# Fused attention and mixer: x and u turned by DMA transposes instead of TensorE matmuls, one DMA transpose for q and k of a pair, other quotas

## The chip, the cores and the metric

The kernel runs on one core of a Trainium2 chip. The metric is the device time of one execution in microseconds (us). The engines have short names in the profile: PE is TensorE (matmuls), PEld its weight loads, DVE is VectorE, ACT is ScalarE, POOL is GpSimd and SP is SyncE, which issues DMAs. POOL issues DMAs too. Sixteen DMA engines serve all queues.

## What is computed

Eight batches (b = 0 to 7), eight heads, 576 tokens, head width 64. Causal attention over 16 beacon keys and 576 keys gives x of shape 8 x 576 x 512; x then goes through a mixer over tokens and a two-layer MLP:

```
scores = q @ k_all.T / 8, masked;  a = softmax(scores);  x = a @ v_all
h = x.T @ U @ V                      # U: 576 x 32, V: 32 x 576, over tokens
u = x + h.T
out = u + relu(u @ w_ch1) @ w_ch2    # 512 -> 2048 -> 512
```

Inputs and output are float32; the kernel works in float16 with float32 sums in PSUM.

## The kernel before

**Attention.** A *pair* is two heads of one batch: p = 4b + c, with c = 0 to 3, so 32 pairs. For a pair, `regroup` (L216) copies q and k on DVE into a tile `pr`, tokens on the partitions. From batch 3 on (`HB = 3`), `turn_pair` (L248) has SP turn these with two DMA transposes, one for k and one for q, into `raw`, and `order_units` (L256) copies each on DVE into its place in `qT` and `kT`. For the batches before, `qkT_units` turns them on PE (L229, L231). `score_units` makes the scores in two visits of PE (L286), each followed by exps on ACT (L292), and then the masks on DVE (L273, L275). `av_unit` multiplies with v (L310) and writes x, scaled, into `xb` on DVE (L318, L319): tokens on the partitions, 5 groups of 112, 128, 128, 128 and 80 tokens by 512 channels.

**Mixer.** The MLP needs u with channels on the partitions, the tile `uT` (4 chunks `cc` of 128 channels by all 4608 tokens). `mix_units` (L323) gives a `head` (x times U, L339) and two `part`s, of 240 and 336 tokens. A part fills four PSUM tiles `ups`, one for each cc. When `turned` is false, 20 matmuls a batch with the identity put x itself, turned, into `ups` (L354), four matmuls with V add h (L364), and the sum is copied into `uT`, two copies on ACT (L374) and two on DVE (L372). When `turned` is true, DMA transposes (L324) have written x into `uT` before, the 20 matmuls fall away, and all four results are added to `uT` on DVE (L370).

`mix(b)` sets `turned` to `b >= NF and len(queue) >= LAG + 5`, with `NF = 2` and `LAG = 12`. At the calls the queue holds 12, 8, 7, 6, 5, 4 and 3 units for b = 1 to 7, so it is false each time: all eight batches go through the identity.

**MLP.** `uT` is cut into nine blocks of 512 tokens. `mlp_units` (L378) gives 32 units of four matmuls for a block: 16 `g_unit`s (first layer, L397, with a relu on ACT or DVE) and 4 x 4 `c_unit`s (second layer, L413). The residual u needs tokens on the partitions again: four DMA transposes of `uT` into `ut` (L387), issued at the first g unit, and an add on DVE (L426). For block 0, `turned` is false: u is added by 16 identity matmuls (L421), and the result is copied by DVE (L430) and ACT (L428).

**Order of the work.** It is written out by hand (`tc.manual_schedule`): each engine works through its instructions in the order in which the Python code emits them. Attention is emitted pair by pair; between its seven steps `fill` pops units from a queue of MLP and mixer units, evenly, `quota` of them in a pair (9; 4 in batch 2, by `QUOTA`). `feed(b)` appends the blocks that batch b completes. `mix(b)` puts the mixer units ahead of them: the first `LAG` units of the queue when `turned` (2 or none otherwise), the head, up to three units, the first part, up to three units, the second part, up to three units. For b = 0 and 1 `mix(b)` is called behind the last pair of the batch, for b = 2 to 6 at the first pair of the next batch, for b = 7 at the end; behind pair 7 (the end of batch 1) come 16 units with no attention between them (`AHEAD`). What is still in the queue after pair 31 runs as a tail of MLP alone.

So a batch's last pair, its mixer and the first MLP block that needs it follow each other in one stream on PE, and a late `uT` holds up the first `gps` matmul of that block.

**Queues.** SP issues in order: the outputs (L431, each waits for the DVE's or ACT's `ob`), the transposes of q and k (L244 once a batch, L253 twice a pair) and those of u (L387). POOL issues the loads of q, k and v, which convert float32 to float16 and are cut into small packets: v of the next batch as soon as the last pair of a batch has released its buffer, and q and k of two batches ahead right behind.

Of the kernel before, what the change touches and what calls it, by code (L numbers as in the profile page):

```python
# [17 lines left out]
P = 128  # L18
# [9 lines left out]
def kernel(  # L28
# [187 lines left out]

    def regroup(L, c, i, copy):

        t = pairs.tile([P, 4, 2, D], F16, name=f"pr{i}", tag=f"pr{i}")
        copy(out=t, in_=by_token(L[1][i][:, 2 * c : 2 * c + 2, :]))  # L220
        return t

    def qkT_units(L, pr, qT, kT, c):
# [3 lines left out]
        def one(i, dst, w):  # L227
            ps = pst([P, SK], F16, name="tps")
            nc.tensor.transpose(ps[:, 0:NL], L[0][i][:NL, hs, :], ident[:NL, :NL])  # L229
            for j in range(4):  # L230
                nc.tensor.transpose(ps[:, ds(NL + P * j, P)], pr[i][:, j, :, :], ident)  # L231
# [16 lines left out]
    def turn_pair(pr):  # L248

        out = []  # L250
        for i in range(2):
            t = raws.tile([P, 4, P], F16, name=f"raw{i}", tag=f"raw{i}")
            nc.sync.dma_start_transpose(out=t, in_=pr[i].rearrange("p j h d -> p (j h d)"))  # L253
            out.append(t)
        return out

    def order_units(raw, qT, kT, c):

        def one(i, dst, w):
            nc.vector.tensor_copy(  # L260
                out=dst[:, c, w - 4 * P : w].rearrange("x (p j) -> x p j", j=4),
                in_=raw[i].rearrange("x j p -> x p j"),
            )
# [42 lines left out]
    def av_unit(b, h, ex, vs, xb):  # L306
# [14 lines left out]
        )  # L321

    def mix_units(xb, u0, turned=True):  # L323


        cell = {}

        def turn():
            for j in range(NT):
                nc.sync.dma_start_transpose(  # L330
                    out=uT[:, :, ds(u0 + q0[j], nq[j])], in_=xb[: nq[j], j, :]
                )

# [41 lines left out]

        return turn, head, [lambda: part([0, 1]), lambda: part([2, 3, 4])]

# [126 lines left out]
    def group_first(c, i, copy):  # L504

        prs.setdefault(c, []).append(regroup(Ls[0], c, i, copy))
        hs = SETS[c]
        copy(out=Ls[0][0][i][:NL, hs, :], in_=raw["head"][:NL, i, hs, :])

    def regroup_of(p):  # L510
        b, c = divmod(p, NH2)
        prs[p] = [regroup(Ls[b], c, i, nc.vector.tensor_copy) for i in range(2)]

# [45 lines left out]
    AHEAD = 16  # L559
    LAG = 12  # L560
    HINT = 5

    FIRST = [0, 0, 0, 0, 10, 5, 4, 4]

    QUOTA = {2: 4}

# [35 lines left out]
    with tc.manual_schedule(engines={ENG.PE, ENG.Activation, ENG.DVE, ENG.SP, ENG.Pool}):  # L602
# [41 lines left out]
        for p in range(NP1):  # L644
# [37 lines left out]
        for p in range(NP1, NP):  # L682
# [84 lines left out]
    with tc.If(n_bad != 0, label="general"):  # L767
        with tc.For_i(0, B, 1) as bi:
# [4 lines left out]
            for c in range(NH2):  # L773
                pr = [regroup(L, c, i, nc.vector.tensor_copy) for i in range(2)]
# [4 lines left out]
            _, head, parts = mix_units(xb, 0, False)  # L779
            head()  # L780
# [36 lines left out]
```

## Time and profile before

| | us |
|---|---|
| median of 3 runs (lowest to highest) | 368.31 (367.41 to 369.45) |
| the profiled execution | 367.15 |
| its span in the profile | 365.5 |
| outside the span | 1.65 |
| PE busy | 349.8 |
| MLP matmuls, L397 and L413, busy | 135.7 + 134.4 |
| x through the identity on PE, L354, busy | 11.6 (160 matmuls) |
| copies of `ups` to `uT`: DVE L372, ACT L374 | 13.1, 11.5 |

The page's busy times are unions: a matmul's own duration (379 ns for 512 columns) overlaps the next one's, so the time that matmuls take in the stream is read from the start of one group to the start of the next in the timeline. In the timeline each row is a run of like instructions: start, length, engine, line, operation, out<-in, count, and in brackets the idle time ahead of it with what ended it. The table of stretches gives for each stretch the busy time of each engine and the granted share of the TensorE clock (PEclk).

### The profile page before, as it was taken

Reading aid. Unit: us, or ns where it says so; the run is one execution under the profiler, and the core shown is the slowest. Engines: PE = TensorE matmul, PEld = TensorE weight load, DVE = VectorE, ACT = ScalarE, POOL = GpSimd, SP = SyncE. Lnnn points to the kernel's source line nnn. Section 1 sums busy time; section 2 is a strip of 40 time slices with the busy share of each in tenths; the row PEclk is TensorE's granted clock in tenths of the full one; section 3 lists DMA queues with packets and bytes.
Section 4 is the critical chain, followed back from the end, with each engine's and each line's share of the span. In section 5 each row is a group of like instructions: output and inputs, shape, how many; then the busy total and the mean of one; then the engine's idle time right before and its main releaser. Section 6 shows DMA issues by size and latency. Waiting matters only on the chain.

```text
span 365.5 us, 7721 instructions
## 1 busy us (share of the span) xinstructions
PE 349.8 (96%) x3040; PEld 173.5 (47%) x3040; DVE 204.7 (56%) x565; ACT 173.7 (48%) x382; POOL 83.9 (23%) x123
## 2 busy tenths in 40 slices
PE   7777999999999999999999999999999999999995
PEld 3544545545545444544445444544454555444442
DVE  4887664357776675565666666756566446223311
ACT  3976660177654553466436643674356503401300
POOL 8976436400336001800081005000000000000000
PEclk9989999999999999999999999999999999999999
DMA  9999999990999952999299917942141013013112
GB/s 178 212 151 184 194 201 156 176 170 10 145 136 163 178 80 59 121 190 137 60 111 206 131 35 101 150 74 41 63 120 26 2 57 103 14 59 87 31 44 79
DMA packets 117916, 40.52 MB, mean 111 GB/s; under 512 B 93680, under 2 KB 112112, under 8 KB 117872
## 3 DMA queue, kind: packets, MB, share of 16 engines
q0 software_dynamic: 65904, 17.54, 54.4%
q1 hardware_dynamic: 51520, 22.12, 31.0%
q8 instruction: 25, 0.41, 0.5%
q10 hardware_dynamic: 448, 0.30, 0.3%
q14 instruction: 19, 0.16, 0.1%
HBM read 37.86 MB, written 9.44 MB: 129 GB/s over the span
## 4 chain that ended last, share of the span: by engine, by line
PE 85%; DMA 6%; DVE 3%; ACT 2%; POOL 2%; issue 0%; DVEq 0%; POOLq 0%
PE cps L413 34%; PE gps L397 33%; PE po L310 6%; PE sps L286 6%; DMA w<-in_moe_w_ch_dram 2%; DMA raw<-pr 2%; PE ups L354 2%; DMA st<-in_q_dram 2%; ACT expt L292 2%; PE idle L211 1%; POOL vs L173 1%; DVE gT L403 1%; PE ups L364 1%; PE qtp L339 1%; PE tps L231 1%; DVE expt L273 1%
## 5 line engine op out<-in xcount | busy, mean ns | idle before, releaser
L292 ACT ACTIVATE expt<-sps 128x496 f16<-128x496 f32 (+2 forms) x256 | 111.1, 531 | 61.9 <-PE sps L286 61.7
L397 PE MATMUL gps<-uT,w 128*128 128x512 f16 x576 | 135.7, 379 | 1.8 <-ACT uT L374 1.2
L413 PE MATMUL cps<-w,gT 128*128 128x512 f16 x576 | 134.4, 379 | 0.0
L401 ACT ACTIVATE gT<-gps 128x512 f16<-128x512 f32 x86 | 51.8, 608 | 64.3 <-PE gps L397 62.0
L413 PEld LDWEIGHTS <-gT 128*128 128x128 f16 x576 | 52.3, 98 | 61.1 <-issue 3.7
L397 PEld LDWEIGHTS <-w 128*128 128x128 f16 x576 | 51.8, 98 | 60.8 <-issue 6.1
L403 DVE TENSOR_SCALAR gT<-gps 128x512 f16<-128x512 f32 x58 | 40.1, 691 | 45.7 <-PE gps L397 44.0
L426 DVE TENSOR_TENSOR ob<-cps,ut 128x512 f32<-128x512 f32 x32 | 22.1, 691 | 49.6 <-PE cps L413 49.1
L173 POOL DMA_DIRECT2D vs<-in_v_dram x50 | 40.8, 831 | 14.3 <-DMA st<-in_q_dram 4.9
L310 PEld LDWEIGHTS <-expt 128*128 128x128 f16 (+1 forms) x960 | 36.9, 98 | 15.0 <-DVE expt L273 2.2
L310 PE MATMUL po<-vs,expt 128*128 128x65 f16 (+1 forms) x960 | 40.3, 195 | 1.0 <-DVE expt L273 0.5
L286 PE MATMUL sps<-qT,kT 64*128 64x80 f16 (+4 forms) x384 | 33.4, 286 | 4.0 <-DVE kT L233 3.4
L319 DVE TENSOR_TENSOR xb<-po,rec 128x320 f16<-128x320 f32 x64 | 31.4, 491 | 2.2
L374 ACT ACTIVATE uT<-ups 128x240 f16<-128x240 f32 (+1 forms) x32 | 11.5, 416 | 39.3 <-PE ups L364 39.2
L273 DVE TENSOR_TENSOR expt<-expt,bigmask 128x512 f16<-128x512 f16 x64 | 26.7, 418 | 6.0 <-ACT expt L292 5.9
L163 POOL DMA_DIRECT2D vs<-in_beacon_v_dram x10 | 5.4, 538 | 100.6 <-PE po L310 100.3
L318 DVE RECIPROCAL rec<-po 128x5 f32<-128x5 f32 x64 | 12.0, 187 | 27.0 <-PE po L310 26.2
L286 PEld LDWEIGHTS <-kT 64*128 64x128 f16 x384 | 12.3, 95 | 30.1 <-issue 10.8
L372 DVE CAST uT<-ups 128x240 f16<-128x240 f32 (+1 forms) x32 | 13.1, 450 | 8.5 <-PE ups L364 8.5
L220 DVE COPY pr<-st 128x512 f16<-128x512 f16 x56 | 14.2, 296 | 1.0 <-DMA st<-in_q_dram 0.6
L260 DVE COPY qT<-raw 128x512 f16<-128x512 f16 x20 | 12.4, 619 | 2.7 <-DMA raw<-pr 2.7
L275 DVE TENSOR_TENSOR expt<-expt,mask 80x80 f16<-80x80 f16 x64 | 12.5, 196 | 0.0
(65 smaller groups left out, 157.2 us busy)
## 6 DMA issues: line engine op xcount, KB each, us to landing
out_dram<-ob SPq DMA_DIRECT2D x36, 256.0 KB, 2.3
w<-in_moe_w_ch_dram POOLq DMA_DIRECT2D x4, 1024.0 KB, 11.5
st<-in_k_dram POOLq DMA_DIRECT2D x6, 512.0 KB, 10.0
st<-in_q_dram POOLq DMA_DIRECT2D x6, 512.0 KB, 13.4
vs<-in_v_dram POOLq DMA_DIRECT2D x18, 128.0 KB, 7.5
stm<-in_k_dram SPq DMA_DIRECT2D x4, 256.0 KB, 4.6
vs<-in_v_dram POOLq DMA_DIRECT2D x12, 64.0 KB, 6.2
stm<-in_q_dram SPq DMA_DIRECT2D x3, 256.0 KB, 5.7
```

What stands on the lines that cost most here:

```text
L173: nc.gpsimd.dma_start(out=dst[a : a + nq[j], j, :, :], in_=src[hs, ds(q0[j], nq[j]), :].rearrange("h p d -> p h d"))
L220: copy(out=t, in_=by_token(L[1][i][:, 2 * c : 2 * c + 2, :]))
L273: nc.vector.tensor_tensor(out=e4, in0=e4, in1=bigmask, op=ALU.min)
L286: nc.tensor.matmul(ps[g, i][:, ds(o, w)], kT[hp, c, ds(P * ch, P)], qT[hp, c, ds(qa, w)], start=True, stop=True,)
L292: nc.scalar.activation(out=ex[i][:, ds(SLOT * g, gw[g])], in_=ps[g, i][:, 0 : gw[g]], func=AF.Exp, scale=scale)
L310: nc.tensor.matmul(po[:, j, :], ex[0 : nk[c], ds(blk[(c, j)], P)], vs[0 : nk[c], ds(c * H * E + h * E, E)], start=(c == 0), stop=(c == j),)
L319: nc.vector.tensor_tensor(out=xb[:, :, ds(h * D, D)], in0=po[:, :, 0:D], in1=r.broadcast_to([P, NT, D]), op=ALU.mult)
L397: nc.tensor.matmul(g[:, 0:n], w1[:, cc, ts(dc, P)], uT[:, cc, ds(t0, n)], start=(cc == 0), stop=(cc == NCC - 1))
L401: nc.scalar.activation(out=gT["t"][:, dc, 0:n], in_=g[:, 0:n], func=AF.Relu)
L403: nc.vector.tensor_scalar_max(out=gT["t"][:, dc, 0:n], in0=g[:, 0:n], scalar1=0.0)
L413: nc.tensor.matmul(ps[:m, :], gT["t"][:, dc, ds(P * i, m)], w2[:, dc, :], start=(dc == 0), stop=turned and dc == NDC - 1, skip_group_check ...
L426: nc.vector.tensor_tensor(out=ob[:m, :], in0=ps[:m, :], in1=gT["u"][:m, i, :], op=ALU.add)
```

## The change

Four things, told with the lines of the kernel before where there are such:

- `mix(b)` sets `turned = b > 0`. For b = 1 to 7 x is turned by ten DMA transposes from SP: five (one for each token group) of channels 0 to 383, issued behind the third pair of the batch, and five of channels 384 to 511, issued in `mix(b)`. `LAG` is 8. The two parts' results are added to `uT` on DVE.
- Block 0 takes u from DMA transposes as the others do.
- q and k of a pair share one tile `pr` and one DMA transpose of 128 x 1024, in place of two of 128 x 512.
- The quota is 6 in batch 3 and 8 in batch 7 (4 in batch 2 as before, else 9).

```diff
-    def regroup(L, c, i, copy):
-        t = pairs.tile([P, 4, 2, D], F16, name=f"pr{i}", tag=f"pr{i}")
-        copy(out=t, in_=by_token(L[1][i][:, 2 * c : 2 * c + 2, :]))
-        return t
+    def pair_tile():
+        return pairs.tile([P, 2, 4, 2, D], F16, name="pr", tag="pr")
+    def regroup(L, c, i, copy, pr):
+        copy(out=pr[:, i, :, :, :], in_=by_token(L[1][i][:, 2 * c : 2 * c + 2, :]))
...
     def turn_pair(pr):
-        out = []
-        for i in range(2):
-            t = raws.tile([P, 4, P], F16, name=f"raw{i}", tag=f"raw{i}")
-            nc.sync.dma_start_transpose(out=t, in_=pr[i].rearrange("p j h d -> p (j h d)"))
-            out.append(t)
-        return out
+        t = raws.tile([P, 2, 4, P], F16, name="raw", tag="raw")
+        nc.sync.dma_start_transpose(
+            out=t.rearrange("x i j p -> x (i j) p"), in_=pr.rearrange("p i j h d -> p (i j h d)")
+        )
+        return t
...
+    def turn_x(xb, u0, c0, c1):
+        for j in range(NT):
+            nc.sync.dma_start_transpose(
+                out=uT[:, c0:c1, ds(u0 + q0[j], nq[j])], in_=xb[: nq[j], j, P * c0 : P * c1]
+            )
...
-    LAG = 12
+    LAG = 8
-    QUOTA = {2: 4}
+    QUOTA = {2: 4, 3: 6, 7: 8}
...
-                mlp_units(512 * t, 512, lambda i, m, t=t: rows[ds(512 * t + P * i, m), :], t % 2, t > 0)
+                mlp_units(512 * t, 512, lambda i, m, t=t: rows[ds(512 * t + P * i, m), :], t % 2)
...
-        turned = b >= NF and len(queue) >= LAG + 5
-        turn, head, parts = mix_units(xbs[b], S * b, turned)
+        turned = b > 0
+        head, parts = mix_units(xbs[b], S * b, turned)
         if turned:
-            turn()
-        n = LAG if turned else 2 if b >= NF else 0
+            turn_x(xbs[b], S * b, NH2 - 1, NH2)
+        n = LAG if turned else 0
...
+            if c == NH2 - 2 and b > 0:
+                turn_x(xbs[b], S * b, 0, NH2 - 1)
...
+            if c == NH2 - 2:
+                turn_x(xbs[b], S * b, 0, NH2 - 1)
```

The first of the last two places is in the loop over the pairs of batches 0 and 1, the second in the loop over the others.

More of the change, by code (lines that the diff above doesn't have):

```diff
@@ L261, in one @@
                 out=dst[:, c, w - 4 * P : w].rearrange("x (p j) -> x p j", j=4),
-                in_=raw[i].rearrange("x j p -> x p j"),
+                in_=raw[:, i, :, :].rearrange("x j p -> x p j"),
             )
@@ L374, in part @@
                     nc.scalar.activation(out=dst, in_=ups[cc], func=AF.Copy)
-        return turn, head, [lambda: part([0, 1]), lambda: part([2, 3, 4])]
+        return head, [lambda: part([0, 1]), lambda: part([2, 3, 4])]
     def mlp_units(t0, n, dst, flip, turned=True):
@@ L504, in group_first @@
     def group_first(c, i, copy):
-        prs.setdefault(c, []).append(regroup(Ls[0], c, i, copy))
+        if c not in prs:
+            prs[c] = pair_tile()
+        regroup(Ls[0], c, i, copy, prs[c])
         hs = SETS[c]
@@ L511, in regroup_of @@
         b, c = divmod(p, NH2)
-        prs[p] = [regroup(Ls[b], c, i, nc.vector.tensor_copy) for i in range(2)]
+        prs[p] = pair_tile()
+        for i in range(2):
+            regroup(Ls[b], c, i, nc.vector.tensor_copy, prs[p])
     for i in range(2):
@@ L773 @@
             for c in range(NH2):
-                pr = [regroup(L, c, i, nc.vector.tensor_copy) for i in range(2)]
+                pr = pair_tile()
+                for i in range(2):
+                    regroup(L, c, i, nc.vector.tensor_copy, pr)
                 for u in qkT_units(L, pr, qT, kTs[0], c):
@@ L778 @@
                 safe_head(h, qT, kTs[0], vss[0], xb)
-            _, head, parts = mix_units(xb, 0, False)
+            head, parts = mix_units(xb, 0, False)
             head()
```

7 lines of the change are left out of this document (1 added, 6 removed).

## The prediction

> **What bounds the kernel.** I read the page's head first, then its 40 slices, then who waited for whom, then the timelines of PE, DVE and SP around the mixer of a batch.
>
> ```profile
> span 365.5 us, 7721 instructions
> PE 349.8 (96%) x3040; PEld 173.5 (47%) x3040; DVE 204.7 (56%) x565; ACT 173.7 (48%) x382; POOL 83.9 (23%) x123
> PE   7777999999999999999999999999999999999995
> DMA  9999999990999952999299917942141013013112
> ```
>
> PE is busy 96% of the span. The table of stretches says where the rest lies: 8.8 us before 34.9 us, 4.1 us behind the last attention pair (297 us on, nearly all of it the end), 2.7 us in the 262 us between. So from 35 to 297 us a matmul taken off PE's stream is worth its full place in the stream, and any wait put into it costs in full. DVE and ACT have room on the mean. The DMA engines do not: up to about 210 us they are busy most of the time (9 is 90% or more).
>
> What x costs on PE is read from the timeline of PE, batch 4's mixer:
>
> ```profile
> 191.94 0.60 PE L354 MATMUL ups<-ident,xb 112*128 112x112 f16 x8
> 192.47 0.28 PE L364 MATMUL ups<-Vsb,qts 32*128 32x240 f16 x4
> ...
> 194.03 0.77 PE L354 MATMUL ups<-ident,xb 128*128 128x128 f16 x12
> 194.73 0.32 PE L364 MATMUL ups<-Vsb,qts 32*128 32x336 f16 x4
> ```
>
> From start to start the eight take 0.53 us and the twelve 0.70: 1.23 us a batch.
>
> **What goes.** The built order of the changed kernel has 312 fewer rows on PE: 140 matmuls of L354 and 16 of L421, each with its weight load.
> - L354 for b = 1 to 7: 7 x 1.23 = 8.6 us.
> - L421: in the same timeline four of them stand at 59.60 and what follows at 59.92 or, at the other three places, 0.22 us later (69.18 to 69.40). 4 x 0.22 = 0.9 us.
> - Two waits of `gps` for `uT`, at 119.33 (0.53 us) and 158.11 us (0.67), 1.2 us in all by PE's waits. Both belong to the form in which a part stands right ahead of the block that needs it; I count them off here and set the new waits in full below.
>
> All of it lies on PE's full stretch: -10.7 us. The ACT copies that go (L374, 7 x 4) and the halved count of `raw` transposes free engines that do not bound: nothing. The identity transposes of q and k for batches 0 to 2 stay. The quotas move units between batches and the tail (70 units in the queue at the end before, 86 after); PE is full in both, so nothing, as long as a pair with six units still covers ACT (four exps of 1.96 us and four of 1.53 us, about 3.5 us) and DVE. With PE at 6 x 0.87 + 2.3 us = 7.5 us a pair it does; batch 2 already runs with four.
>
> **What is added on DVE.** All eight adds of a batch are now DVE's. Two copies of 240 take 0.71 us together there, two of 336 take 0.92, so one more costs 0.32 and 0.42 us: four adds take 1.3, then 1.7 us. (An add that reads PSUM and SBUF takes what a copy does: L426 691 ns for 512, L430 the same.) On the mean DVE stays under 65%. But two batches have no units left between the parts and the next block's first g unit, and there the chain of adds lies on the path:
> - b = 1 (no attention beside it). The queue gives: part 0, c unit, part 1, g1.0. From the end of part 0 on PE: DVE adds 1.3, the `ob` add 0.6, the adds of part 1 1.7, so the last is done at 3.7 and g1.0 ends at 4.0; undisturbed it ends at 0.87 + 0.25 + 0.94 = 2.1. Cost 2 us.
> - b = 2, pair 13, quota 6: second score visit, head, masks, part 0, k's order copy, part 1, av, g2.0. DVE has the masks ahead of the adds, and the masks wait for four exps (1.6 us behind the visit). Then 0.9 masks, 1.3, 0.5, 1.7: the last add at 6.0, g2.0 ends at 6.2. Undisturbed: 0.4 + 0.22 + 0.25 + 0.46 + 0.94 = 2.3. Cost 4 us.
> - b = 3 to 6: nine and more units between part 1 and the g unit, b = 7 five. The adds are covered: nothing.
>
> The rows in which DVE shows this order today, ahead of the wait at 119.33 (DVE's timeline):
>
> ```profile
> 112.84 0.41 DVE L273 TENSOR_TENSOR expt<-expt,bigmask 128x512 f16<-128x512 f16 x1
> ...
> 114.24 0.71 DVE L372 CAST uT<-ups 128x240 f16<-128x240 f32 x2
> ...
> 118.86 0.92 DVE L372 CAST uT<-ups 128x336 f16<-128x336 f32 x2
> ```
>
> **What is added on SP and the DMA engines.** Ten transposes a batch, 35 KB to 98 KB each. No row shows an issue of 128 or 384 channels, or of 1024. Every issue of 512 columns takes 1.2 us on SP, with 64 rows (L244) as with 128, and lands 2.4 us after its start where the DMA engines are idle. Either the columns set it (0.3, 0.9, 2.4 us) or each takes 1.2; I take half way for the last five (0.65, 3.3 us for five), 1 us for the first. Landing beside POOL's loads is much later, and POOL loads v exactly when a batch's last pair has ended, which is when SP issues the last five:
>
> ```profile
> L253 SPq DMA_TRANSPOSE raw<-pr x2: 1276/1276/1277, 146.5 to 147.9; - x2
> DMA to landing us min/median/max: 7.6/8.5/9.5
> ```
>
> This is the tile `raw` asked for alone at 146 to 150 us; at 107 to 111 us it is 6.4 to 7.0, at 185 to 188 us 5.3 to 6.6, from 264 us on 2.4.
> - When are they due? b = 3: part 0's adds come eight units, the head, three units and most of two pairs' attention behind, 13.7 us after pair 16 starts; part 1's 18.5. The issue of the first two ends at about 1 (regroup) + 2 (raw) + 1.3 = 4.3, plus 8.5 to 9.5 landing: 13 to 14. Just in time; b = 4 to 6 have shorter landings, b = 7 no loads.
> - b = 1: last x at 58.5 us, issue done by 62.2, landing 4 to 6.7 (what `ut` and `ob` take at 60 to 80 us): 66 to 69; part 0 is due at 68. b = 2: the adds are held to about 119 and 121 us by the masks anyway, x lands 118 to 122. I set 0.5 us for all of them together; the bounds are 0 and the 3 us by which a landing of 12 us would be late at each of b = 1 to 5.
> - Pair 14's `raw` stands on SP behind the first five of b = 2 (issued at about 102.7 us, when xb is ready): 102.8 now, 107.7 then, landed 111 to 113, while DVE's order copy comes at 109.4 and has masks and k's copy behind it, which pair 13's scores need. Pair 13 begins at 113.4 and needs them at 2.5 us behind the landing, 113.5 to 115.5: 1 us (bounds 0 and 3). Later batches have a pair of 10 us to cover this.
> - Single transposes for q and k save SP nothing or 1.2 us a pair, and DVE's q copy waited for the second one before as well: nothing.
>
> **A cold clock.** The longest idle time of PE behind its start-up is 1.56 us (before 22.65 us), and the clock falls behind it:
>
> ```profile
> 18.00:22.00 4.00, 2.53 (x44) 1.59 (x43) 3.33 (x11) 3.51 (x9) 2.55 (x5) 1.00 1.60 183
> 22.00:26.00 4.00, 3.35 (x39) 1.89 (x39) 3.58 (x13) 1.84 (x6) 3.52 (x6) 0.69 1.50 140
> 26.00:30.00 4.00, 3.21 (x60) 2.24 (x56) 3.25 (x12) 2.97 (x8) 4.00 (x10) 0.89 1.14 106
> ```
>
> (start and end, length, busy time of PE, PEld, DVE, ACT, POOL, then PEclk.) 4 x 0.31 + 4 x 0.11 = 1.7 us of clock lost. The new wait at b = 2 is longer than that one, but PE is full ahead of it: I set half, 0.8 us; bounds 0 and 2 x 1.7.
>
> The Trainium skill, "TensorE: Matmul & The Clock Gate", Part 1 (What's actually happening), gives a rule for it: the array falls to half its clock after one idle window of about 3.4 us. By it only b = 2's wait would be long enough, and only if av does not break it; the row above, with 1.56 us idle, speaks for an earlier fall than the rule. By the rule the sum would be 0.8 us lower, by the row 0.9 us or more higher.
>
> **The sum.** -10.7 + 2 + 4 + 0.5 + 1 + 0.8 = -2.4 us. The profiled execution's own 367.15 (span 365.5 and 1.65 around it) would become 364.75, the median of 368.31 becomes **365.9 us**, 0.65% less. The start, the end and what lies around the span stay.
>
> **The rivals.**
> - *The new waits are smaller than worked out.* If g2.0 does not wait the whole chain out, or the clock holds and nothing is late, -10.7 + 2 + 2 to 4 leaves 361.5 to 363.7; I set 362.5. For it: DVE has idle time beside every part; against it: the built order has masks ahead of the adds.
> - *x lands late in the loaded windows, and DVE, which works in order, stands still with masks, `ob` and relus behind the add.* This is the case that ends slower. Its place is b = 2 to 5, the pairs beside POOL's loads; it decides from a landing of 9.5 us for the second of the last five, which is what `raw` shows today at 147.9 us, without 2304 more packets a batch behind and beside it. Another 512 or so in the same window, at the pace of the two above (1.9 us more landing for the second), put x at about 12 us: 3 us late, at four batches, 12 us: 365.9 + 12 = 378 us; with only two batches late 372. For it: the DMA row at 9; against it: the loads end about 20 us into a batch, and 8 to 11 units lie between.
> - The Trainium skill, "DMA: Bandwidth & Descriptors", Queues, rings and completion order, says that each DMA engine takes turns between queues by packets, so transposes go on beside a full load queue at a share of the pace. The landings of 5 to 10 us against 2.4 agree; a share, not a full wait, speaks against the 378.
> - *That the change does not do it* (`turned` false, as before) is excluded by the 312 rows.
>
> **How the numbers follow.** Forecast 0.50 (364 to 368.5: six tenths of it over 0.5% faster, the rest within); smaller waits 0.25 (faster); late landings 0.25 (slower in all but a tenth). 0.5%, 1.8 us, is about what a measurement of this kernel can tell from no change. So faster 0.54, same 0.23, slower 0.23. The range is 361.5 to 374: it leaves out the late landings at three and more batches, and the case with no wait at all (357.6).
>
> **What would show it.** L354 at 20 matmuls and L421 gone. PE waits at g1.0 (about 2 us) and g2.0 (about 4 us) for the DVE add into `uT`, near 69 and 119 us; PEclk below 1 behind the latter. `uT<-xb` landings of 6 to 10 us at the start of batches 3 to 6, and adds that wait for them by less than 1 us. PE full from 130 us on, 1.2 us a batch shorter. It is wrong if DVE waits for `uT<-xb` by microseconds in several batches, or if g2.0 does not wait.

## The result, and the profile after

The changed kernel takes 380.82 us (379.23 to 381.68, 4 runs), the kernel before 367.90 on the same chip: a ratio of 1.034, with an interval of 1.029 to 1.039. It is slower by 12.9 us; the forecast was 365.9, the range 361.5 to 374.0. The times of this document are medians over all executions, while the ratios leave out executions over 1.5% slower than the fastest of their kernel. The profiled execution took 380.61 us with a span of 378.9.

Line numbers of the changed kernel differ a little: L326 issues the transposes of x, L252 those of `raw`, L388 those of `ut`; L371 adds into `uT`, L260 copies `raw` into order, L340 and L346 make `qts`, L365 adds h; L398 and L414 are the two MLP layers, L286 the scores, L310 a @ v, L427 the `ob` add.

The head of the page and three rows of its 40 slices (PE, the clock, the DMA engines), to be laid beside those of before:

```profile
span 378.9 us, 7523 instructions
...
PE 349.6 (92%) x2884; PEld 167.0 (44%) x2884; DVE 216.3 (57%) x596; ACT 162.3 (43%) x351; POOL 83.6 (22%) x123
...
PE   7677998689996789999999999999999999999995
...
PEclk9999999969999669999999999999999999999999
...
DMA  9999999999999963999599939553422312203202
```

PE does 156 matmuls less and is as long busy as before (349.6 against 349.8 us). A busy time that stays while work goes means a slower clock, and the row PEclk shows it: a 6 in slice 9, two in slices 14 and 15, each behind a slice (8 and 13) in which PE has a 6. The balance of the span closes: the matmuls removed are worth 8.6 + 0.9 = 9.5 us by the prediction's rows; PE's busy time fell by 0.2, so the clock cost 9.3; PE's idle time rose from 15.7 to 29.3 us, 13.6 more. -9.5 + 9.3 + 13.6 = +13.4 us, from 365.5 to 378.9. From slice 16 on both rows are clean. (The 9.5 are of the prediction's rows, so the 9.3 is an estimate, and the highest of three; the other two, 6.6 and 7.8, are worked out below.)

The table of stretches of the changed kernel says the same in four rows (columns as before: start and end, length, PE, PEld, DVE, ACT, POOL with counts, PEclk, DMA share, GB/s):

```profile
34.90:73.10 38.20, 35.75 (x305) 17.49 (x306) 19.04 (x51) 11.61 (x25) 10.12 (x13) 1.00 1.75 162
73.10:106.70 33.60, 29.59 (x258) 14.27 (x257) 23.34 (x70) 19.04 (x42) 12.15 (x17) 0.90 2.15 152
106.70:145.50 38.80, 31.01 (x273) 14.03 (x272) 22.93 (x65) 15.64 (x35) 8.89 (x11) 0.82 1.18 143
145.50:310.00 164.50, 163.27 (x1409) 77.30 (x1408) 106.14 (x284) 79.86 (x172) 22.04 (x28) 1.00 0.81 109
```

The same stretches of the kernel before:

```profile
34.90:73.10 38.20, 37.66 (x342) 19.49 (x343) 19.42 (x54) 14.12 (x31) 18.17 (x24) 1.00 1.73 183
73.10:106.70 33.60, 32.62 (x321) 16.19 (x320) 23.87 (x73) 23.23 (x51) 4.83 (x8) 1.00 1.07 117
106.70:145.50 38.80, 38.27 (x347) 18.87 (x347) 24.07 (x66) 20.22 (x45) 9.38 (x12) 1.00 1.05 120
```

So nearly everything is lost in two places, at the mixers of b = 1 and b = 2; the mixers of b = 3 to 6 lie in the last row of the changed kernel, at full clock and 99% busy (that of b = 7 begins at 308.58). PE's timeline at the first place, the end of batch 1 (last column: idle time ahead and what ended it):

```profile
72.52 0.32 PE L365 MATMUL ups<-Vsb,qts 32*128 32x336 f16 x4
75.78 1.44 PE L398 MATMUL gps<-uT,w 128*128 128x512 f16 x3 [2.94 <-DMA uT<-xb]
78.52 0.58 PE L398 MATMUL gps<-uT,w 128*128 128x512 f16 x1 [1.30 <-DVE uT L371]
```

and at the second, pairs 12 and 13:

```profile
125.21 0.98 PE L286 MATMUL sps<-qT,kT 64*128 64x496 f16 x4 [5.41 <-DVE kT L260]
...
131.61 1.09 PE L365 MATMUL ups<-Vsb,qts 32*128 32x240 f16 x8 [0.40 <-DVE qts L346]
133.28 0.80 PE L310 MATMUL po<-vs,expt 128*128 128x65 f16 x15 [0.59 <-DVE uT L371]
135.14 1.87 PE L398 MATMUL gps<-uT,w 128*128 128x512 f16 x4 [1.06 <-DVE uT L371]
```

The waits of these six rows make 11.7 us, of 13.6 us of new idle time. The waits for the loads of the MLP weights grew by 2.1: 1.32 us for `w1` at 35 us and 1.33 for `w2` at 59, where the kernel before waits 0.58 for `w1`.

The longest wait, 5.41 us, is not for x at all: it is pair 13's scores waiting for the ordering copies of `raw`. (The code makes scores one pair ahead, `scores_of(p + 1)`: "pair 13's scores" are those made in pair 13's turn, and they belong to pair 14. That is why they need pair 14's `raw`.) DVE's timeline and SP's show why:

```profile
122.57 0.59 DVE L260 COPY qT<-raw 128x512 f16<-128x512 f16 x1 [7.52 <-DMA raw<-pr]
```

```profile
107.93 6.39 SPq L326 DMA_TRANSPOSE uT<-xb  x5
114.43 2.26 SPq L252 DMA_TRANSPOSE raw<-pr  x1
```

Pair 14's `pr` was ready at 107.9 us (its regroup: 107.43, 0.48 us for both copies), but SP was issuing five transposes of x until 114.3; `raw` went out at 114.43 (102.8 in the kernel before; 5.2 us of the difference are the lateness of the whole stream from batch 1 on) and needed 8.1 us to land, at 122.6. DVE stood for 7.52 us with the masks and k's copy behind that instruction, and PE for 5.41. The transposes themselves (the line's rows by operation):

```profile
L326 SPq DMA_TRANSPOSE uT<-xb x70: 1172/1246/2255, 55.6 to 307.2; - x70
```

Smallest, median and largest issue in ns: 128 and 384 channels cost the same 1.25 us (five of 384 take 6.39 us from 107.93 on, five of 128 take 6.46 from 120.13 on). `raw`, now 1024 columns, has a median of 1260 ns, where 512 columns had 1216. So the price of an issue on SP does not go with its size; single issues took up to 2.4 us (`raw`) and 3.4 (`ut`), pair 14's own 2.26.

The gain itself is read from a steady batch, from the first matmul of one head to that of the next. Before it is 38.79 us (188.53 to 227.32), in the changed kernel 38.36 (200.11 to 238.47): 0.43 us less, and not 1.23. The first row is the kernel before, the second the changed one:

```profile
188.53:227.32 38.79, 38.77 (x349) 19.06 (x349) 25.05 (x65) 20.33 (x45) 8.62 (x12) 1.00 1.00 120
200.11:238.47 38.36, 37.93 (x330) 17.91 (x329) 25.38 (x68) 18.80 (x41) 5.08 (x6) 1.00 1.10 138
```

PE's busy time falls by 0.84 us there. At this rate the change takes 7 x 0.84 + 0.9 = 6.8 us of work off PE, and the clock costs 6.6 us. PE's timeline at batch 4's first part:

```profile
204.17 0.48 PE L286 MATMUL sps<-qT,kT 64*128 64x336 f16 x8
204.58 0.28 PE L365 MATMUL ups<-Vsb,qts 32*128 32x240 f16 x3
205.29 0.26 PE L365 MATMUL ups<-Vsb,qts 32*128 32x240 f16 x1 [0.43 <-ACT expt L292]
205.48 2.77 PE L414 MATMUL cps<-w,gT 128*128 128x512 f16 x12
```

The four matmuls that stay take 0.90 us here, where four of L364 took 0.22 in the prediction's timeline: 0.43 us of it is a wait for an exp on ACT, which has to release a PSUM tile; the rest is no wait that the trace names. In the kernel before, the part stands elsewhere: twelve MLP matmuls lie between the score visit and the part's matmuls at 191.94.

```profile
188.93 0.48 PE L286 MATMUL sps<-qT,kT 64*128 64x336 f16 x8
189.34 2.76 PE L413 MATMUL cps<-w,gT 128*128 128x512 f16 x12
```

With `LAG` at 8 the part of batches 4 and 5 falls right behind a score visit, whose exps still run, and no identity matmuls fill the time. In batch 6, where four MLP matmuls lie between (281.41), the four L365 do not wait. No run has one of the two without the other, so what share each has is not shown.

What the waits do to the clock is read from stretches of 4 us:

```profile
120.00:124.00 4.00, 0.00 (x0) 0.00 (x0) 1.43 (x6) 0.00 (x0) 0.49 (x1) 0.91 1.52 210
124.00:128.00 4.00, 2.79 (x22) 1.38 (x23) 2.83 (x9) 1.96 (x4) 0.00 (x0) 0.50 1.46 173
...
136.00:140.00 4.00, 4.00 (x26) 1.55 (x25) 3.08 (x9) 1.96 (x4) 0.00 (x0) 0.50 0.64 98
```

The second 0.50 comes behind the three short waits at g2.0, the first g unit of block 2 (0.40, 0.59, 1.06 us; g1.0 is that of block 1), and PE is full at half clock for 4 us. With the stretches between (0.73 and 0.69), the next one (0.95) and those at the first place (0.50 and 0.71 from 76 to 84 us) the shares missing add up to 2.42 stretches, 9.7 us at the most, as PE was idle in part of them. With each missing share weighted by PE's busy time in its stretch it is 7.8 us. The three estimates put the clock's cost at 6.6 to 9.3 us.

### The profile page after: what moved, and what is told of

It is laid out like the page before. It is cut to its first block, busy times and chain, and to the rows that moved or that the text cites. A ratio compares the mean times of both kernels' runs of the same rounds, so it can differ in the third digit from the quotient of the medians.

```text
span 378.9 us, 7523 instructions
## 1 busy us (share of the span) xinstructions
PE 349.6 (92%) x2884; PEld 167.0 (44%) x2884; DVE 216.3 (57%) x596; ACT 162.3 (43%) x351; POOL 83.6 (22%) x123
## 4 chain that ended last, share of the span: by engine, by line
PE 74%; DMA 14%; DVE 4%; SPq 4%; ACT 2%; POOL 2%; issue 1%; DVEq 0%; ACTq 0%; POOLq 0%
PE gps L398 33%; PE cps L414 27%; PE po L310 6%; PE sps L286 6%; DMA raw<-pr 4%; SPq L326 3%; DMA uT<-xb 3%; DMA w<-in_moe_w_ch_dram 2%; DMA stm<-in_k_dram 2%; DMA st<-in_q_dram 2%; ACT expt L292 1%; DMA stm<-in_q_dram 1%; POOL vs L173 1%; PE tps L232 1%; DVE expt L273 1%
## 5 line engine op out<-in xcount | busy, mean ns | idle before, releaser
L398 PE MATMUL gps<-uT,w 128*128 128x512 f16 x576 | 139.3, 387 | 6.6 <-DMA uT<-xb 2.9
L414 PE MATMUL cps<-w,gT 128*128 128x512 f16 x576 | 135.5, 383 | 1.3 <-DMA w<-in_moe_w_ch_dram 1.3
L402 ACT ACTIVATE gT<-gps 128x512 f16<-128x512 f32 x85 | 51.0, 609 | 110.9 <-PE gps L398 106.8
L398 PEld LDWEIGHTS <-w 128*128 128x128 f16 x576 | 52.8, 99 | 67.1 <-issue 11.8
L414 PEld LDWEIGHTS <-gT 128*128 128x128 f16 x576 | 52.9, 98 | 65.3 <-issue 8.6
L427 DVE TENSOR_TENSOR ob<-cps,ut 128x512 f32<-128x512 f32 x36 | 24.8, 690 | 50.4 <-PE cps L414 50.1
L310 PEld LDWEIGHTS <-expt 128*128 128x128 f16 (+1 forms) x960 | 37.6, 99 | 17.5 <-issue 4.0
L310 PE MATMUL po<-vs,expt 128*128 128x65 f16 (+1 forms) x960 | 40.9, 196 | 2.0 <-ACT expt L292 0.7
L286 PE MATMUL sps<-qT,kT 64*128 64x80 f16 (+4 forms) x384 | 33.6, 287 | 8.8 <-DVE kT L260 5.6
L286 PEld LDWEIGHTS <-kT 64*128 64x128 f16 x384 | 12.2, 94 | 35.6 <-issue 9.8
L371 DVE TENSOR_TENSOR uT<-ups,uT 128x240 f16<-128x240 f32 (+1 forms) x56 | 21.8, 449 | 7.9 <-PE ups L365 4.9
L260 DVE COPY qT<-raw 128x512 f16<-128x512 f16 x20 | 11.9, 595 | 12.5 <-DMA raw<-pr 12.5
L260 DVE COPY kT<-raw 128x512 f16<-128x512 f16 x20 | 12.0, 600 | 0.0
## 6 DMA issues: line engine op xcount, KB each, us to landing
st<-in_k_dram POOLq DMA_DIRECT2D x6, 512.0 KB, 10.3
```

What stands on the lines that cost most here:

```text
L260: nc.vector.tensor_copy(out=dst[:, c, w - 4 * P : w].rearrange("x (p j) -> x p j", j=4), in_=raw[:, i, :, :].rearrange("x j p -> x p j"),)
L286: nc.tensor.matmul(ps[g, i][:, ds(o, w)], kT[hp, c, ds(P * ch, P)], qT[hp, c, ds(qa, w)], start=True, stop=True,)
L310: nc.tensor.matmul(po[:, j, :], ex[0 : nk[c], ds(blk[(c, j)], P)], vs[0 : nk[c], ds(c * H * E + h * E, E)], start=(c == 0), stop=(c == j),)
L398: nc.tensor.matmul(g[:, 0:n], w1[:, cc, ts(dc, P)], uT[:, cc, ds(t0, n)], start=(cc == 0), stop=(cc == NCC - 1))
L402: nc.scalar.activation(out=gT["t"][:, dc, 0:n], in_=g[:, 0:n], func=AF.Relu)
L414: nc.tensor.matmul(ps[:m, :], gT["t"][:, dc, ds(P * i, m)], w2[:, dc, :], start=(dc == 0), stop=turned and dc == NDC - 1, skip_group_check ...
```

## The experiments

Two theories. **Queue:** SP issues in order, x takes ten issues of 1.25 us a batch, and five of them stand ahead of `raw`; the remedy is another order or fewer issues. **Contention:** what is late is the landing, 8 to 11 us beside POOL's loads where 2.4 us is the idle figure; the order matters little, and the remedy is to have no transposes there. The kernel before was timed beside each of the four groups of runs: 367.32, 367.37, 368.59 and 368.47 us. These differ by 1.3 us, so a gain of about a microsecond between runs of different groups is not told from none.

### Which batches: x by DMA from batch 3 on

```diff
-        turned = b > 0
+        turned = b > 2
-        n = LAG if turned else 0
+        n = LAG if turned else 2 if b >= NF else 0
...
-            if c == NH2 - 2:
+            if c == NH2 - 2 and b > 2:
                 turn_x(xbs[b], S * b, 0, NH2 - 1)
```

The first five of b = 1 go too; the rest of the change stays. The edit also puts the mixers of b = 1 and 2 back to their old place, behind 0 and 2 units of the queue in place of 8.

> x of b = 1 and 2 through the identity again, DMA transposes for b = 3 to 7 alone; the other three parts of the change stay. Queue theory (SP issues in order at 1.25 us per transpose whatever its size; the x of b = 1 and 2 comes late itself and holds up raw of pair 14; PE idles 13.6 us more than before and its clock falls for another 9.3): the loss was in b = 1 and 2 alone, so 367.9 - 5 x 1.23 (L354) - 0.9 (L421) - 0.7 (the wait at b = 3) + about 1.9 (w2 later behind u's transposes) = 362 us, mean clock back at 0.99. Contention theory (every added DMA slows all landings in the loaded windows, in batches 3 to 6 as well): 366 us or more.

366.57 us (363.83 to 369.96, 10 runs), ratio 0.995 (0.990 to 0.999). All of the loss is gone, with 2.5 us of matmuls put back; the clock is 1.00 throughout. Some waits remain: for `w1` (1.08 us) and `w2` (1.78 us; the expectations of later runs call both waits those for w2), and, beside 0.51 us for `kT`, this one ahead of pair 16's scores:

```profile
129.77 0.62 PE L310 MATMUL po<-vs,expt 128*128 128x65 f16 x15 [1.37 <-DVE gT L404]
```

So the transposes of the two early batches, with the place of their mixers, are the cause of the loss. The time is the one set for the contention theory, but not for its reason: no instruction of this run waits for x. The 362 us are not reached: the gain of a steady batch is smaller than 1.23 us, as its rows above showed, and these waits stand against it.

### One of the two batches through the identity

The same edit with `turned = b > 1` (b = 1 through the identity), and with `b > 0 and b != 2` (b = 2).

> Only b = 1 goes back to the identity; b = 2 to 7 by DMA transposes. Queue theory: the wait at g1.0 (72.8 to 79.1 us, 5.2 us) and the slow clock behind it (about 3.4 us) go, 1.2 us of identity matmuls come back: 380.8 - 7.4 = 373.4 us; pair 13's wait of 5.4 us stays. Contention theory: the loads of batch 2 and 3 come earlier too and pair 13's wait shrinks as well, 370 us or less.

375.22 us, ratio 1.021 (1.013 to 1.030): 5.6 us come back. The waits at g1.0 are gone, the one ahead of pair 13's scores is still 4.43 us. Here the stream is not late: the five transposes of x go out at 103.26 us, `raw` of pair 14 at 109.90, POOL's loads from 106.94 on, and `raw` lands in 7.8 us.

> Only b = 2 goes back to the identity. Queue theory: raw of pair 14 is issued some 6 us earlier on SP, pair 13's wait (5.4 us), the waits around g2.0 (about 2 us) and the slow clock behind them (6.5 us) go, 1.2 us of identity matmuls come back: 380.8 - 12.7 = 368 us; the wait at g1.0 stays. Contention theory: v of batch 4 loads at that time anyway, raw lands 6 us or more after its issue, half of the wait stays: 374 us.

371.48 us, ratio 1.010 (1.005 to 1.014): 9.3 us come back by the medians (8.9 by the ratios), between the two expectations. The two places add up: 5.6 + 9.3 = 14.9 us, against the 14.3 us of both together (380.82 - 366.57). With 1.23 us of identity matmuls put back at each, the price of b = 1 is about 6.8 us and that of b = 2 about 10.5.

### How much of it is the clock

Matmuls with the identity into an unused PSUM tile keep PE at work where it would wait: 13 ahead of g1.0, 24 ahead of pair 13's scores. What PE waits for stays as it is.

```diff
+        if b == 1:
+            p1 = parts[1]
+            parts[1] = lambda: (p1(), keep_warm(pst([P, 512], F32, name="idle"), 13))
...
+            if p == 13:
+                keep_warm(pst([P, 512], F32, name="idle"), 24)
```

> The changed kernel with 13 matmuls of 512 columns that nobody reads ahead of g1.0 and 24 ahead of pair 13's second scores, in place of idle time (2.9 and 5.3 us at 0.22 us each). Clock theory (the idle time lets the clock fall to half, and that costs 9.3 of the 24 us lost): the waits stay, PEclk stays at 1 from 72 to 84 us for most of it and from 120 to 141 us, 380.8 - 7 = 374 us. Rival (the clock only falls where PE waits anyway and costs nothing): 381 us or more.

376.72 us, ratio 1.023 (1.014 to 1.032): 4.1 us come back for matmuls that nobody reads, less than the 7 expected. In its stretches of 4 us:

```profile
124.00:128.00 4.00, 3.50 (x31) 1.46 (x29) 3.06 (x11) 1.96 (x4) 0.00 (x0) 1.00 1.46 174
128.00:132.00 4.00, 2.59 (x52) 1.42 (x52) 3.70 (x12) 1.53 (x4) 0.00 (x0) 1.00 1.51 227
132.00:136.00 4.00, 3.01 (x15) 0.80 (x15) 3.82 (x10) 0.65 (x2) 0.00 (x0) 0.69 1.32 187
```

124 to 132 us are at 1.00, where the changed kernel had 0.50 and 0.73. So the fall of the clock is an effect of the idle PE with a price of its own. The 0.69 comes at g2.0, behind its short waits. Weighted by PE's busy time as before, 2.9 us of clock are still lost in this run, 4.9 less than in the changed kernel, where 4.1 were measured.

### Block 0's u through the identity

```diff
-                mlp_units(512 * t, 512, lambda i, m, t=t: rows[ds(512 * t + P * i, m), :], t % 2)
+                mlp_units(512 * t, 512, lambda i, m, t=t: rows[ds(512 * t + P * i, m), :], t % 2, t > 0)
```

> The changed kernel with block 0's u by identity matmuls again. Queue theory: the four u transposes at 34 us do no harm on SP, which is idle then; what they cost is the load of w2, which lands 1.3 us late for PE. 0.9 us of matmuls come back, 1.3 us of wait go, and the loads of batch 2 land a little earlier: 380 us (379 to 381). Contention theory: the transposes of 0.5 MB slow the load queue for a long stretch (q and k of batch 2 took 20 to 26 us to land in place of 12 to 15), x of b = 1 lands late because of it: 377 us or less.

376.54 us, ratio 1.022 (1.015 to 1.029): 4.3 us come back, although block 0's four transposes are issued at 34 us and batch 1's x only from 55.6 on. The last five of batch 1's x land in 5.8 to 7.7 us and not in 8.5 to 10.6, and PE's waits at g1.0 shrink from 2.94 and 1.30 us to 0.59 and 0.36. The transposes at 34 us cannot block SP at 62. In the changed kernel the loads of batch 2's q and k, issued by POOL at 44 to 50 us, take 20 to 26 us to land (12 to 15 before): the loads were set back, and x met them. This is contention, at a distance of 20 us; that the set-back loads are the link is read from the landings and not tried by itself.

### Another order on SP: `raw` first

```diff
             if p + 3 < NP and p + 3 >= HB * NH2:
                 turn_of(p + 3)
+            if c == NH2 - 1:
+                turn_x(xbs[b], S * b, 0, NH2 - 1)
...
-            if c == NH2 - 2:
-                turn_x(xbs[b], S * b, 0, NH2 - 1)
```

> The changed kernel with the first five x transposes of b = 2 to 7 put on SP behind the next pair's raw instead of ahead of it. Nothing is added or taken away. Queue theory: raw of pair 14 is issued at about 108 us instead of 114.4, before v of batch 4 loads (111.6), and lands by 112; pair 13's wait of 5.4 us and some 3 us of slow clock go: 372.5 us. Contention theory: it lands late beside the loads in any case: 378 us or more.

378.14 us, ratio 1.025 (1.013 to 1.037). Pair 14's `raw` goes out at 106.56 us and lands in 4.6, and pair 13's scores (at 118.55) do not wait, where they waited 5.41 us. But pair 15's `raw` now stands behind the five, is issued at 116.25 and lands 11.0 us later. DVE and PE of this run:

```profile
127.25 0.59 DVE L260 COPY qT<-raw 128x512 f16<-128x512 f16 x1 [6.82 <-DMA raw<-pr]
```

```profile
128.70 0.66 PE L365 MATMUL ups<-Vsb,qts 32*128 32x240 f16 x8 [6.49 <-DVE qts L346]
```

`qts` is released by DVE, which stood at the copy ahead of it. The wait moved one `raw` on. The queue theory falls as the whole cause, though the order on SP decides which transfer meets the loads.

### Half as many issues: x in one step

All 512 channels of a token group in one transpose, issued in `mix(b)`: five issues in place of ten.

```diff
-            turn_x(xbs[b], S * b, NH2 - 1, NH2)
+            turn_x(xbs[b], S * b, 0, NH2)
```

(and the two calls for channels 0 to 383 dropped)

> The changed kernel with x in one step: five transposes of 512 channels a batch in mix, none behind the third pair. The same bytes and packets. Queue theory with 1.25 us for an issue of whatever size: SP spends 6.3 us on x of a batch in place of 12.6, raw of pair 14 stands ahead of x, the last x of b = 1 lands some 3 us earlier: 371 us. If the issue time went with the columns, or the packets were what is late, x would be no earlier: 379 us or more.

380.42 us, ratio 1.036 (1.028 to 1.043): nothing is gained. Both `raw`s are early now and x is what is late, landing 8.7 to 9.7 us after its issue:

```profile
126.68 0.62 PE L310 MATMUL po<-vs,expt 128*128 128x65 f16 x15 [2.86 <-DVE uT L371]
132.28 1.86 PE L398 MATMUL gps<-uT,w 128*128 128x512 f16 x4 [4.97 <-DVE uT L371]
```

Whichever transpose is last, PE waits for it.

### The pair's single transpose alone

The kernel before with one tile `pr` and one transpose of 1024 columns for q and k, nothing else.

```diff
-        for i in range(2):
-            t = raws.tile([P, 4, P], F16, name=f"raw{i}", tag=f"raw{i}")
-            nc.sync.dma_start_transpose(out=t, in_=pr[i].rearrange("p j h d -> p (j h d)"))
-            out.append(t)
+        t = raws.tile([P, 2, 4, P], F16, name="raw", tag="raw")
+        nc.sync.dma_start_transpose(
+            out=t.rearrange("x i j p -> x (i j) p"), in_=pr.rearrange("p i j h d -> p (i j h d)")
+        )
```

> The kernel before with one DMA transpose for q and k of a pair, nothing else of the change. An issue of 1024 columns takes what one of 512 takes (1.26 us), so SP gets 1.2 us a pair back, but raw is late for DVE in two places only: 367 us, no change by 0.5%. Rival: q's order copy now waits for k's half too and PE waits at some pairs: 369 us.

369.26 us (366.60 to 372.75, 10 runs), ratio 1.003 (0.999 to 1.008). No difference that shows. The rival's mechanism does not show either: PE waits for k's order copy once, 0.3 us.

### POOL's loads held back

A copy of one element from batch 3's x, behind its first pair, stands on POOL ahead of the loads of v of batch 4 and of q and k of batch 5.

```diff
+                if b != 3:
+                    v_loads(v[b + 1], beacon_v[b + 1], vss[(b + 1) % 2], ALLH)
+            if b == 3 and c == 1:
+                nc.gpsimd.tensor_copy(out=hold, in_=xbs[3][0:1, 0, D : D + 1])
+                v_loads(v[4], beacon_v[4], vss[0], ALLH)
```

> The changed kernel, with POOL held back by one small copy that reads batch 3's x after its first pair: the loads of v of batch 4 and of q and k of batch 5 are issued at about 122 us and not from 111.6 us on, so that the transposes of raw(14) and of batch 2's x land without loads beside them. The order on SP stays. If the landing beside the loads is the cause of b=2's waits (contention), raw(14), issued at 114.4 us, lands in 3 to 4 us and not 8.1, the 5.41 us wait ahead of pair 13's scores falls under 1.5 us, and with the clock that comes back the time is 372 to 375 us. If the queue on SP is the cause (raw issued at 114.4 and not at 102.8), landing matters little: over 4 us of the wait stay, and the time is 379 or more.

380.81 us, ratio 1.033 (1.026 to 1.041): no gain, and the mechanism shows nevertheless. Pairs 14 and 15's `raw` land in 3.2 and 3.4 us (last row of the tile between 110 and 127 us), and pair 13's scores wait 1.86 us and not 5.41:

```profile
DMA to landing us min/median/max: 3.2/3.3/3.4
```

The loads, issued from 123.2 us on, then meet block 2's four u transposes, which land in 7.7 to 12.7 us, and PE gets a new wait:

```profile
142.46 0.98 PE L310 MATMUL po<-vs,expt 128*128 128x65 f16 x15 [3.63 <-DVE gT L404]
```

Here the waits were moved once more, so the time cannot tell the theories apart. The next run takes the loads out.

### Without these loads

Batch 4 computes with the old v and batch 5 with constant q and k, set by POOL; 11 transfers between 111 and 132 us fall out.

```diff
+                if b != 3:
+                    v_loads(v[b + 1], beacon_v[b + 1], vss[(b + 1) % 2], ALLH)
...
+                else:
+                    for t in Ls[5][0] + Ls[5][1]:
+                        nc.gpsimd.memset(t, 0.125)
```

> The changed kernel without the loads of v of batch 4 (its old contents are used) and of q and k of batch 5 (POOL sets these tiles to a constant), so batches 4 and 5 compute on other data; 11 transfers of POOL fall out between 111 and 132 us. Order and number of the transposes on SP stay. Contention: raw(14) is issued at 114 us still, lands in 3 to 4 us, the wait ahead of pair 13's scores falls under 2 us, no wait comes up in its place in batch 3, and the time is 371 to 375 us (of batch 2's 9.3 us only the adds' 2.2 us at g2.0 and some of the clock are left). Queue: less than 2 us go, 379 or more.

373.98 us (373.50 to 376.88, 4 runs), ratio 1.020 (1.013 to 1.026): 6.8 us come back by the medians, 5.3 by the ratios (1.034 and 1.020), with SP's order unchanged. (0.9 us of this is a shorter wait at g1.0, 1.91 and 1.43 us in place of 2.94 and 1.30; it lies ahead of the loads taken out and is not their effect.) SP's timeline and PE's:

```profile
107.11 6.67 SPq L326 DMA_TRANSPOSE uT<-xb  x5
113.89 2.45 SPq L252 DMA_TRANSPOSE raw<-pr  x1
```

```profile
121.00 0.58 PE L286 MATMUL sps<-qT,kT 64*128 64x496 f16 x4 [1.16 <-DVE kT L260]
...
128.60 1.84 PE L398 MATMUL gps<-uT,w 128*128 128x512 f16 x4 [1.24 <-DVE uT L371]
```

`raw` is issued as late as before (113.89), but lands in 4.4 us: 1.16 us of wait, not 5.41, and PEclk is 0.96 between 106.7 and 145.5 us, not 0.82. This is the contention theory's figure (371 to 375). Of the roughly 10.5 us of b = 2, half to two thirds are the landing beside loads with the clock that it costs; what is left is the 6.7 us on SP's queue (1.16 us of wait) and the adds at g2.0 (0.40, 0.59 and 1.24 us).

### The quotas

The changed kernel with `QUOTA = {2: 4}`, as before the change.

> The changed kernel with the quotas of before ({2: 4}, so 9 units a pair in batches 3 and 7). Longer pairs in batch 3 leave more cover for raw and for batch 2's x: if the shorter pairs of the new quotas are part of the cause, the wait ahead of pair 13's scores (which lies in pair 12's time, quota 6 now, 9 then) falls by 2 us or more and the time is 376 to 378 us. If the quotas are no part of it, the time is 380 to 382 us, as the queue is only eaten earlier.

395.77 us (394.73 to 400.79), ratio 1.073 (1.066 to 1.080): 14 to 15 us worse than the changed kernel, where 376 to 382 had been expected. From 106 us on `gps` waits seven times for `uT`, 10.0 us; between 145.5 and 310 us PE is busy for 153.44 us in place of 163.27. PE and DVE at the mixer of b = 3:

```profile
172.79 1.44 PE L398 MATMUL gps<-uT,w 128*128 128x512 f16 x3 [1.80 <-DVE uT L371]
175.68 2.29 PE L398 MATMUL gps<-uT,w 128*128 128x512 f16 x5 [1.45 <-DVE uT L371]
```

```profile
171.51 0.41 DVE L371 TENSOR_TENSOR uT<-ups,uT 128x240 f16<-128x240 f32 x1 [1.50 <-DMA uT<-xb]
175.12 0.51 DVE L371 TENSOR_TENSOR uT<-ups,uT 128x336 f16<-128x336 f32 x1 [1.55 <-DMA uT<-xb]
```

At the calls of `mix` for b = 3 to 7 the queue holds 7, 6, 5, 4 and 3 units; with the change's quotas it holds 19, 18, 17, 16 and 19. The twelve units that batch 3's smaller quota leaves over are the cover between the issue of x and its use, kept up to the end. With them no instruction waits for x from b = 3 on; without them the adds wait for x in b = 2 to 5, by up to 1.94 us at once, and for b = 7 in the tail by 2.10.

### Versions meant to be the best

x by DMA from batch 3 on, u of block 0 through the identity, and the quotas of before:

> x by DMA only from batch 3 on (as in the run from batch 3 on, 366.57 us), u of block 0 by identity again, and the quotas of before. That run's profile still had 2.86 us of waits for w2 and 1.88 us for gT ahead of pair 16's scores. If these are what is left of the change's price, and end with the small transposes of block 0 and the short pairs, the time is 366.6 - 2.9 - 1.9 + 1.2 (block 0's identity matmuls) = 363 us, under both kernels by over 1%. If the waits only move on, 366 us or more.

383.77 us, ratio 1.038 (1.029 to 1.047): about 16 us over the run from batch 3 on (ratios 1.038 and 0.995), as with the quotas alone (between 145.5 and 310 us PE is busy for 153.31 us). With the change's quotas:

> x by DMA from batch 3 on only, u of block 0 by identity, the change's quotas (4, 6 and 8). Against the run from batch 3 on (366.57 us), 2.86 us of waits for w2 should go and 1.2 us of identity matmuls come back: 364 to 365 us if those waits were a price of the small transposes at 34 us; 366.5 to 368 if w2 is late anyway.

366.64 us (364.97 to 369.67, 10 runs), ratio 0.998 (0.994 to 1.001). The wait for `w1` stays (1.01 us), that for `w2` goes. 1.85 us of waits go there and 1.0 for `gT`, 1.5 come up for `kT`, 1.2 us of identity matmuls come back, and the time is the same. And x from batch 4 on (`turned = b > 3`, u of block 0 through the identity):

> The same with x by DMA from batch 4 on: batch 3's x costs 1.23 us of matmuls more, and its transposes no longer stand beside batch 3's loads and u transposes. If x of batch 3 costs waits of its own (raw of pair 16 was late in the run from batch 3 on, 1.88 us of PE), 0.5 us less than the run from batch 3 on with u of block 0 by identity; if that wait has nothing to do with x, 1.2 us more than it.

365.98 us (364.98 to 367.27, 10 runs), ratio 0.994 (0.991 to 0.998). It cannot be told from the two runs with x from batch 3 on. The waits around pair 16 stay without any transpose of batch 3's x (1.15 us for `gT`, 0.51 for `kT`), so that x is not their cause; `raw` of pair 16 lands in 10.0 and 10.3 us in these two runs, issued 2 to 3 us behind the last of POOL's loads of that time. What these versions gain over the kernel before is about half a per cent, the most that any run here gave.

## Why the prediction was wrong, step by step

- **"L354 for b = 1 to 7: 7 x 1.23 = 8.6 us": mis-sized.** The matmuls went, but a steady batch is only 0.43 us shorter. From batch 3's head to batch 4's it is 39.65 us before and 38.15 after, 1.50 less with the old wait of 0.67 us in it, so 0.83 by itself. I took a start-to-start time off the stream as if nothing else would show in its place, and as if the parts kept their places; with `LAG` at 8 two of them stand right behind a score visit and wait for its exps. With 0.43 to 0.83 us a batch the whole change had 3 to 6 us to win there, not 8.6, which fits with the best runs staying within 1% of the kernel before.
- **"No row shows an issue of 128 or 384 channels ... I take half way": mis-sized.** 0.65 and 1 us were set, each is 1.25. Five of them hold SP for 6.4 us and not for 3.3 to 5. The bound that I named ("each takes 1.2") was the truth; the rows of before, 64 rows and 128 at the same 1.2 us, had left the columns open. "Every issue" was too strong as well: in the kernel before one issue of `raw` takes 2.18 us and one of `ut` 2.78. And the transposes of x move 20 to 98 KB, not 35 to 98.
- **"Pair 14's raw ... 1 us (bounds 0 and 3)": the step that failed.** It was 5.41 us. I had `raw` issued at 107.7 us and landed in 3.3 to 5.3 us (at 111 to 113), though the row for issues at 107 to 111 us, 6.4 to 7.0, stood in the same paragraph: with it `raw` lands at 114.1 to 114.7 and the scores wait for 3.2 to 3.8 us, beyond my bound of 3. It took 8.1 us, beside POOL's loads. Of the issue at 114.4, 5.2 us are the lateness of the whole stream, in which the loads (111.6 for 106.05) moved along; 1.5 are the five issues that took 6.4 us and not 5. In the run with b = 1 through the identity, where the stream is not late, the wait is still 4.43 us; without those loads it is 1.16, near the 1 us of the sum. DVE, in order, stood for 7.52 us with the masks and k's copy behind.
- **"x late ... 0.5 us for all of them together": wrong place.** No batch from 3 on was late, where I put the danger. b = 1, which has 16 units and no attention behind it, was: 2.94 us for x itself. I had the issue of its last five done by 62.2 us; it was done at 69.1, since SP was busy with the first five until 62.1 (they wait for pair 6, at 55.6). They landed 8.5 to 10.6 us after their issue (I had 4 to 6.7), and the chain of adds came behind. Part of that is block 0's transposes of u, which I had counted as a pure gain of 0.9 us: with them the loads of batch 2 land later, and without them 4.3 us come back. The sum had nothing for the loads of `w1` and `w2` either, and PE waits 2.1 us more for them.
- **The chains of adds at g1.0 and g2.0 (2 and 4 us): the mechanism was right**, the second one half as long (0.40 + 0.59 + 1.06 us); the first cannot be told from the late x ahead of it, and where x came earlier (block 0's u through the identity) g1.0 waited 0.59 + 0.36 us.
- **"A cold clock ... half, 0.8 us": mis-sized by the most.** It was 6.6 to 9.3 us, by the three estimates above. I priced one wait at the row of before; there were waits of 1 to 5 us at two places, and the clock stood at 0.50 to 0.73 for 8 us behind the first and 16 us behind the second. The Trainium skill, "TensorE: Matmul & The Clock Gate", Part 1 (What's actually happening), has the clock halved after an idle window of about 3.4 us. The wait of 5.41 us agrees (0.50 between 124 and 128 us). The run without the loads does not: its clock is at 1.00 up to 128 us and at 0.68 from 128 to 132, behind 0.40, 0.59 and 1.24 us of waits, 2.2 us in all with work between them.
- **"The quotas ... so nothing": wrong as a step**, though the sum did not show it. I looked at what a pair covers, not at the queue's length at `mix`. They are worth 14 to 15 us.
- **The rival "late landings"** had the right kind of loss in the wrong batches. With the old quotas DVE's waits for x came in b = 2 to 5, as that rival has it. That its 378 us lie near the measured 380.8 is luck: it counted 12 us of late x at four batches, and most of the loss was a late `raw`, a late x at b = 1 and the clock. The sum failed because each term was priced by itself, while the late issue, the loaded landing, DVE's order and the clock came together at the same two places.

## What to carry to other kernels

A DMA transpose that takes a few hundred ns of matmuls off the bound engine needs its landing time *beside the loads of that moment* as cover, plus one fixed issue for each transpose ahead of it in the queue; count the units of other work between issue and use, place by place, and leave the places without cover on TensorE. When such a wait is moved by another order on the queue, look for the next transfer that is then last before calling it gone. Price a new idle time of TensorE at more than its length: here 6.6 to 9.3 us of clock (estimates) came on top of 13.6 us idle. These rules are drawn from this kernel alone.

## What the runs showed of the hardware

- A DMA transpose is issued in about 1.25 us on SP (median) for 128x128, 128x384, 128x512 and 128x1024 alike (1.33 us for 128x512 in the run with x in one step), with single issues of up to 3.6 us (one `raw` in the run with the loads held back), while an output of 256 KB takes SP 0.34 us (median of 36 in the changed kernel). The Trainium skill, "Advanced Engine Details and Errata", X-Bar Transpose (TRN2), calls transposes as fast as regular DMAs; for SP's time that is not so here.
- A transpose of x lands in 2.3 us at the least and one of 1024 columns in 3.0, and both in 8 to 11 us beside POOL's converting loads, and these loads suffer too: 20 to 26 us for batch 2's q and k, where it was 12 to 15.
- Three waits of 0.40, 0.59 and 1.24 us within 4 us brought the granted clock from 1.00 to 0.68 over the next 4 us (the run without the loads); the same waits in the run with the idle matmuls, 0.69. The rows of the first:

```profile
124.00:128.00 4.00, 2.25 (x51) 1.26 (x48) 3.58 (x11) 1.53 (x4) 0.00 (x0) 1.00 0.29 87
128.00:132.00 4.00, 3.32 (x22) 1.14 (x22) 3.48 (x10) 1.00 (x3) 0.00 (x0) 0.68 0.75 173
```
